# Linear attention into a gated feed-forward layer: q times kv on row halves of the TensorE array, and another order of the first two batches

## Chip, core and metric

The kernel runs on one core of a Trainium2 chip. The metric is the device time of one execution in microseconds (us). In the text, TensorE is PE in the profile, with its weight loads as PEld; VectorE is DVE, ScalarE is ACT, GpSimd is POOL, and SyncE, which issues most transfers, is SP. PSUM is the memory of eight banks that TensorE writes.

## What is computed

Attention is linear: there is no softmax. For every batch and head, k and v give a 64 x 64 matrix, q is multiplied by it, and every row of the result is divided by its root mean square. The result goes, heads side by side, as x into a gated feed-forward layer. The weights come as 64-bit floats.

```python
# q, k, v: (8 batches, 8 heads, 576, 64);  tokens: 8 * 576 = 4608, d_model 512, d_ff 1536
kv = np.einsum('bhsd,bhse->bhde', k, v)
out = np.einsum('bhsd,bhde->bhse', q, kv)
rms = np.sqrt(np.mean(out * out, axis=-1, keepdims=True) + 1e-06)
x = out / rms * g_norm                      # then (B,H,S,D) -> (B*S, H*D)
gate = 1.0 / (1.0 + np.exp(-(x @ w_gate)))
val = x @ w_val
y = gate * val @ w_out
```

## The kernel before

**Pairs.** Attention goes by pairs of heads: four pairs per batch, 32 in all. `attention(n)` (L202) gives eleven steps for pair n: KV (12 matmuls, a head on each half of the array's columns), KV_OUT (copy to SBUF; it also issues the loads of k and v for pair n + 2), Q (six transposes of q), Q_OUT (copy; issues the load of q for pair n + 2), U (q times kv), U_SQUARE, U_SUM, U_ROOT, U_NORM (square, sum of squares, root, reciprocal and product), X (six transposes back) and X_OUT (scaled by g_norm into `xT`). TensorE does KV, Q, U and X; ScalarE Q_OUT, U_SQUARE, U_ROOT and X_OUT; VectorE KV_OUT, U_SUM and U_NORM. In U (L233), both heads of a pair stand in one 128 x 128 matrix `kvs`, zero outside two 64 x 64 blocks on its diagonal, so six matmuls with 128 rows and 128 columns do both heads.

**Chunks and blocks.** Tokens go in nine chunks of 512. A plain block of the first layer (`plain`, L361, class `Plain`) takes one chunk c and one slice f of 128 hidden columns: eight matmuls of 128 x 512 (gate and value), a sigmoid on ScalarE (`gate`) and a product on VectorE (`end`), both of them issued during the block after. Chunks 0 and 1 run in plain blocks; later chunks run in another form of the first layer (`first_layer_fast`, L457), which the change leaves alone. `second_layer` (L315) multiplies with w_out and stores.

**Weights.** A unit of weights (1 MB of 64-bit floats: gate and value slices of one f, or two slices of w_out) is loaded by `load_unit` into one of three staging buffers and made 32-bit by seven VectorE operations, `s0` to `s6` (L119 to L160), after one `Abs` on ScalarE (`take_abs`). The last one issues the load of unit u + 3. `converted(u)` issues what is left of the operations up to unit u; `convert_some(n)` issues the next n.

**Order.** Each engine works in the order in which the program issues; nothing is moved. All eight pairs of batches 0 and 1 come first, in rounds (`stage`, L386) in which three pairs are at different steps:

```python
    def stage(i, n_convert):
        do(i, KV, KV_OUT, Q, Q_OUT)
        do(i - 2, U_SUM, U_ROOT, U_NORM)
        do(i - 3, X, X_OUT)
        do(i - 1, U, U_SQUARE)
```

This phase has PSUM buffers of its own (two for KV, one for Q and X, two for U). Block (0, 0) runs among the last rounds. Then PSUM is handed over to four buffers of two banks (`two`), and blocks of chunk 0 and 1 alternate with six conversion operations in each. Attention of the later batches is fed, one step at a time, into slots between the matmuls of later layers.

Of the kernel before, what the change touches and what calls it, by code (L numbers as in the profile page):

```python
# [10 lines left out]
FP32 = mybir.dt.float32  # L11
# [3 lines left out]
ALU = mybir.AluOpType  # L15
# [8 lines left out]
def kernel(  # L24
# [48 lines left out]
    def load_q(n):  # L73
        if n >= B * NHP:
            return
        b, h0 = n // NHP, 2 * (n % NHP)
        t = sb.tile([NP, NJ, 2, HD], FP32, tag="q", name="q")
        for e in range(2):
            nc.sync.dma_start(out=t[:, :, e, :], in_=q[b, h0 + e].rearrange("(p j) d -> p j d", j=NJ))
        pairs[n]["q"] = t  # L80


# [108 lines left out]
    for kv in kvs:  # L191
        nc.vector.memset(kv, 0.0)


    xT = {}
# [6 lines left out]
    def attention(n, at_ps):  # L202

        b, m = divmod(n, NHP)
        d = {}

        def kv_mm():
            d["kv"] = ps = at_ps("kv")
            for j in range(NJ):
                js = slice(HD * j, HD * j + HD)  # L210
                for e in range(2):
                    nc.tensor.matmul(ps[HD * e:HD * e + HD, 0, 0:HD], pairs[n]["k"][:, e, js], pairs[n]["v"][:, e, js],  # L212
                                     start=(j == 0), stop=(j == NJ - 1))

        def kv_out():
            for e in range(2):
                es = slice(HD * e, HD * e + HD)
                nc.vector.tensor_copy(out=kvs[n % 2][es, es], in_=d["kv"][es, 0, 0:HD])
            load_kv(n + 2)

        def q_mm():
            d["q"] = ps = at_ps("qx")
            for j in range(NJ):
                c0 = NP * (j % JH)
                nc.tensor.transpose(ps[:, j // JH, c0:c0 + NP], pairs[n]["q"][:, j].rearrange("p e d -> p (e d)"),  # L225
                                    ident[0:NP, 0:NP])

        def q_out():
            d["qT"] = sb.tile([P, 2, JH * NP], FP32, tag="qT", name="qT")
            nc.scalar.copy(out=d["qT"], in_=d["q"][:, :, 0:JH * NP])  # L230
            load_q(n + 2)

        def u_mm():  # L233

            ps = at_ps("u")
            d["u"] = ps[0:NP, :, 0:JH * P]
            for j in range(NJ):
                c0 = P * (j % JH)
                nc.tensor.matmul(ps[0:NP, j // JH, c0:c0 + P], d["qT"][:, j // JH, NP * (j % JH):NP * (j % JH) + NP],  # L239
                                 kvs[n % 2], start=True, stop=True)  # L240

        def u_square():
            d["sq"] = sb.tile([NP, 2, JH * P], FP32, tag="sq", name="sq")
            nc.scalar.activation(out=d["sq"], in_=d["u"], func=AF.Square)

        def u_sum():
            d["ms"] = sb.tile([NP, 2, 2 * JH], FP32, tag="ms", name="ms")
            nc.vector.tensor_reduce(out=d["ms"].rearrange("p i n -> p (i n)"),
                                    in_=d["sq"].rearrange("p i (n d) -> p (i n) d", d=HD), axis=AX.X, op=ALU.add)

        def u_root():
            nc.scalar.activation(out=d["ms"], in_=d["ms"], func=AF.Sqrt, bias=eps[0:NP], scale=1.0 / HD)  # L252

        def u_norm():
            nc.vector.reciprocal(d["ms"], d["ms"])
            d["xn"] = d["sq"]
            nc.vector.tensor_tensor(out=d["xn"].rearrange("p i (n d) -> p i n d", d=HD),  # L257
                                    in0=d["u"].rearrange("p i (n d) -> p i n d", d=HD),
                                    in1=d["ms"].unsqueeze(3).to_broadcast([NP, 2, 2 * JH, HD]), op=ALU.mult)

        def x_mm():
            d["x"] = ps = at_ps("qx")
            for j in range(NJ):
                c0 = NP * (j % JH)
                nc.tensor.transpose(ps[:, j // JH, c0:c0 + NP], d["xn"][:, j // JH, P * (j % JH):P * (j % JH) + P],  # L265
                                    ident[0:NP, 0:NP])
# [16 lines left out]
    def slot():  # L283
        if fill:
            fill.popleft()()
# [42 lines left out]
                store(c, t0 + i, ot)  # L328


    def two(kind=None):
        return psum0.tile([P, 2, 512], FP32, tag="two", name="two")

    def early(kind):
        shape, bufs = {"kv": ([P, 1, 512], 2), "qx": ([P, 2, 512], 1), "u": ([P, 2, 512], 2)}[kind]
        return psum_e.tile(shape, FP32, tag=kind, name=kind, bufs=bufs)

    class Plain:


        def __init__(self, c, f, ps):
            self.c, self.f, self.ps = c, f, ps

        def mm(self, i, m):
            nc.tensor.matmul(self.ps[:, i], w[("wg", "wv")[i], self.f][:, m, :], xT[self.c][:, m, :],  # L345
# [12 lines left out]
        while late:  # L358
            late.popleft()()

    def plain(c, f, n_convert):  # L361

        converted(f)
        blk = Plain(c, f, two())
        for at in range(2 * NMT):
            i, m = divmod(at, NMT)
            blk.mm(i, m)
            slot()
# [6 lines left out]
    KV, KV_OUT, Q, Q_OUT, U, U_SQUARE, U_SUM, U_ROOT, U_NORM, X, X_OUT = range(11)  # L375
    psum_ctx = tc.tile_pool(name="psum_e", bufs=1, space=bass.MemoryType.PSUM)
    psum_e = psum_ctx.__enter__()
    NE = 2 * NHP
    a = [attention(n, early) for n in range(NE)]

    def do(n, *steps):
        if 0 <= n < NE:
            for step in steps:
                a[n][step]()

    def stage(i, n_convert):  # L386
        do(i, KV, KV_OUT, Q, Q_OUT)
        do(i - 2, U_SUM, U_ROOT, U_NORM)
        do(i - 3, X, X_OUT)
        do(i - 1, U, U_SQUARE)  # L390
        if i == 0:
            take_abs(0)
        convert_some(n_convert)
        if i + 2 == NE:
            load_unit(1)
            load_unit(2)
# [4 lines left out]
    for m in range(NMT):  # L401
        blk.mm(0, m)
    take_abs(1)
    stage(NE + 1, 1)
    for m in range(NMT):
        blk.mm(1, m)
    stage(NE + 2, 1)
    blk.gate()
    convert_some(1)
    blk.end()  # L410
    psum_ctx.__exit__(None, None, None)
# [125 lines left out]
    def mm_ps():  # L537
        return psum.tile([P, 512], FP32, tag="mm", name="mm", bufs=6)

    def at_ps(kind):  # L540
        return psum.tile([P, 2, 512], FP32, tag="at", name="at")


# [37 lines left out]
```

## Time and profile before

| what | value |
|---|---|
| median of three runs | 1197.71 us (1196.88 to 1198.85) |
| the profiled execution: time, span | 1197.71 us, 1195.9 us |
| mean granted TensorE clock | 0.994 |
| TensorE busy, of the span | 1166.5 us (98%) |
| VectorE busy, of the span | 474.2 us (40%) |
| mean of a 128 x 512 matmul record in a plain block (L345) | 602 ns |
| VectorE product at the end of a plain block (L353) | 0.69 us |
| loading ScalarE's table before a root or a sigmoid | 1.28 us |

A span runs from the first to the last instruction; the time is a little longer than the span. A 32-bit matmul leaves two records on TensorE, so 12 matmuls are x24; a transpose leaves one. Records overlap (their ends are modelled), so costs are taken from start to start. In a group of instructions, the numbers after the bar are busy time and mean duration, then the idle time of the engine before them and what ended it.

### The profile page before, as it was taken

The page shows a single profiled execution, that of the slowest core. Times are in us where ns is not written, and L with a number is a line of the kernel's source. Part 1 is how long each engine was busy: PE and PEld are TensorE (multiplying, and loading weights), DVE is VectorE, ACT ScalarE, POOL GpSimd, SP SyncE. Part 2 cuts the span into 40 slices and gives each one's busy share as a digit, 9 for nine tenths or more (in the row PEclk, how much of TensorE's full clock was granted, in tenths as well). Part 3 has the DMA queues.
Part 4 walks back from the last instruction along what each step waited for, and adds up shares of the span by engine and source line. Part 5 has one row for each costly group of instructions (what it writes and reads, how often), then busy time and mean ns, then how long its engine had stood idle before and what let it go on. Part 6 is the DMA issues. An engine that isn't in the chain of part 4 may idle for free.

```text
span 1195.9 us, 13384 instructions
## 1 busy us (share of the span) xinstructions
PE 1166.5 (98%) x5136; PEld 785.7 (66%) x5136; DVE 474.2 (40%) x845; ACT 298.6 (25%) x569; POOL 242.0 (20%) x342
## 2 busy tenths in 40 slices
PE   5889999999999999999999999999999999999998
PEld 5634444554588748884788558864888478748863
DVE  5479996112045403451244304540445035404420
ACT  3422221221134203330233114320343021102110
POOL 0000001000033303430133103420333025404410
PEclk9989999999999999999999999999999999999999
DMA  9833440220211102110112021110200000010000
GB/s 239 199 104 110 138 141 14 64 72 6 56 40 31 31 26 55 45 30 18 48 32 59 9 56 30 31 36 21 62 8 1 26 9 1 1 27 9 1 9 26
DMA packets 71582, 57.48 MB, mean 48 GB/s; under 512 B 40800, under 2 KB 65376, under 8 KB 71520
## 3 DMA queue, kind: packets, MB, share of 16 engines
q1 hardware_dynamic: 71360, 56.64, 17.9%
q8 instruction: 41, 0.67, 0.3%
q14 instruction: 21, 0.17, 0.0%
q10 hardware_dynamic: 160, 0.00, 0.0%
HBM read 47.19 MB, written 9.44 MB: 47 GB/s over the span
## 4 chain that ended last, share of the span: by engine, by line
PE 95%; ACT 2%; DMA 2%; DVE 1%; issue 0%; SPq 0%; ACTq 0%; DVEq 0%
PE mm L471 42%; PE mm L322 23%; PE two L345 14%; PE two L322 7%; PE at L239 2%; PE at L212 1%; PE at L265 1%; PE at L225 1%; PE u L239 1%; DMA q<-in_q_dram 1%; ACT L252 1%; DMA v<-in_v_dram 1%; PE u L345 1%; DVE sq L257 0%; PE two L239 0%; PE qx L225 0%
## 5 line engine op out<-in xcount | busy, mean ns | idle before, releaser
L454 POOL TENSOR_TENSOR tw<-gv 128x256 f32<-128x256 f32 x168 | 120.5, 728 | 896.6 <-PE mm L471 693.5
L322 PE MATMUL mm<-wo,gv 128*128 128x512 f32 x672 | 290.5, 592 | 0.0
L471 PE MATMUL mm<-sx,tw 128*128 128x256 f32 x1008 | 234.2, 380 | 0.0
L322 PEld LDWEIGHTS mm<-wo,gv 128*128 128x128 f32 x672 | 127.3, 190 | 155.3 <-issue 155.0
L471 PEld LDWEIGHTS mm<-sx,tw 128*128 128x128 f32 x1008 | 188.8, 190 | 24.6
L345 PE MATMUL two<-xT,gv 128*128 128x512 f32 x368 | 162.8, 602 | 3.8 <-DVE gv L353 3.8
L483 DVE TENSOR_TENSOR gv<-mm,p 128x256 f32<-128x256 f32 x84 | 35.7, 425 | 321.5 <-PE mm L471 321.5
L471 PE MATMUL mm<-xT,gv 128*128 128x256 f32 x672 | 159.7, 380 | 1.2 <-ACT sg L327 1.2
L471 PEld LDWEIGHTS mm<-xT,gv 128*128 128x128 f32 x672 | 126.0, 190 | 21.2 <-issue 2.9
L345 PEld LDWEIGHTS two<-xT,gv 128*128 128x128 f32 x368 | 70.4, 193 | 90.2 <-issue 89.7
L454 POOL TENSOR_TENSOR tw<-gv,tw 128x256 f32<-128x256 f32 x168 | 126.3, 772 | 1.1
L322 PE MATMUL two<-wo,gv 128*128 128x512 f32 x192 | 84.6, 594 | 0.0
L327 ACT COPY sg<-mm 128x512 f32<-128x512 f32 x28 | 16.4, 586 | 264.4 <-PE mm L322 264.4
L492 DVE TENSOR_TENSOR gv<-mm,p 128x256 f32<-128x256 f32 x84 | 35.7, 425 | 114.0 <-PE mm L471 114.0
L471 PE MATMUL mm<-sx,gv 128*128 128x256 f32 x336 | 79.9, 381 | 0.0
L471 PE MATMUL mm<-xT,tw 128*128 128x256 f32 x336 | 79.9, 381 | 0.0
L501 ACT ACTIVATE sg<-sg 128x256 f32<-128x256 f32 x84 | 35.0, 417 | 162.9 <-DVE sg L500 161.6
L471 PEld LDWEIGHTS mm<-sx,gv 128*128 128x128 f32 x336 | 63.0, 190 | 8.5
L471 PEld LDWEIGHTS mm<-xT,tw 128*128 128x128 f32 x336 | 63.0, 190 | 8.5
L508 DVE TENSOR_TENSOR gv<-gv,sg 128x512 f32<-128x512 f32 x84 | 66.6, 832 | 0.2
L322 PEld LDWEIGHTS two<-wo,gv 128*128 128x128 f32 x192 | 35.8, 190 | 41.8 <-issue 41.6
L477 ACT COPY p<-mm 128x256 f32<-128x256 f32 x84 | 31.3, 372 | 93.7 <-PE mm L471 93.7
(84 smaller groups left out, 820.6 us busy)
## 6 DMA issues: line engine op xcount, KB each, us to landing
k<-in_k_dram SPq DMA_DIRECT2D x32, 288.0 KB, 3.5
v<-in_v_dram SPq DMA_DIRECT2D x32, 288.0 KB, 4.3
q<-in_q_dram SPq DMA_DIRECT2D x64, 144.0 KB, 3.1
st<-in_moe_w_gate_dram SPq DMA_DIRECT2D x12, 512.0 KB, 3.7
st<-in_moe_w_val_dram SPq DMA_DIRECT2D x12, 512.0 KB, 4.8
st<-in_moe_w_out_dram SPq DMA_DIRECT2D x12, 512.0 KB, 4.4
out_dram<-sg SPq DMA_DIRECT2D x24, 192.0 KB, 2.3
out_dram<-sg SPq DMA_DIRECT2D x24, 128.0 KB, 2.3
```

Source lines behind the costliest of these rows:

```text
L212: nc.tensor.matmul(ps[HD * e:HD * e + HD, 0, 0:HD], pairs[n]["k"][:, e, js], pairs[n]["v"][:, e, js], start=(j == 0), stop=(j == NJ - 1))
L239: nc.tensor.matmul(ps[0:NP, j // JH, c0:c0 + P], d["qT"][:, j // JH, NP * (j % JH):NP * (j % JH) + NP], kvs[n % 2], start=True, stop=True)
L322: nc.tensor.matmul(ps[:, i], gv[c, f][:, ts], w["wo", f], start=(f == 0), stop=(f == NFT - 1))
L327: nc.scalar.copy(out=ot, in_=ps[:, i])
L345: nc.tensor.matmul(self.ps[:, i], w[("wg", "wv")[i], self.f][:, m, :], xT[self.c][:, m, :], start=(m == 0), stop=(m == NMT - 1), skip_grou ...
L454: nc.gpsimd.tensor_tensor(out=tw[f, i], in0=b[in0], in1=b[in1] if isinstance(in1, tuple) else tw[f, in1], op=ALU.subtract)
L471: nc.tensor.matmul(ps, wt[:, m, :], xs[:, m, :], start=(new and m == 0), stop=(m == NK - 1), skip_group_check=True)
L477: nc.scalar.copy(out=d["p1"], in_=pa)
L483: tt(out=d["h"][:, h1], in0=pb, in1=d["p1"], op=ALU.add)
L492: tt(out=d["h"][:, h2], in0=pb, in1=d["p1"], op=ALU.add)
L501: nc.scalar.activation(out=d["sg"][:, h2], in_=d["sg"][:, h2], func=AF.Sigmoid)
L508: tt(out=d["h"], in0=d["h"], in1=d["sg"], op=ALU.mult)
```

## The change

It has two parts. In the first, U takes a head on each half of the array's rows: kv of the first head lies on partitions 0 to 63 and of the second on 64 to 127 (one copy in KV_OUT, no zeros), and twelve matmuls with 64 rows and 64 columns write the two heads to different PSUM banks. The norm then writes the heads back side by side.

In the second, the order at the start is another one. Unit 0 of the weights is loaded ahead of k and v, and the first two q on ScalarE's queue. Unit 0 is converted ahead of attention. The four pairs of batch 0 come next, each round going U to norm of one pair with KV and Q of a later one behind it, and block (0, 0) is spread over the last two. The pairs of batch 1 then run inside blocks 1 to 5 of chunk 0, at fixed places between their matmuls. Blocks of chunk 0 and chunk 1 alternate from f = 6 on, and chunk 1 finishes behind. All these tiles share the four PSUM buffers of two banks.

```diff
-    load_kv(0)
-    load_q(0)
     load_unit(0)
-    load_kv(1)
-    load_q(1)
+    for n in range(2):
+        load_kv(n)
+        load_q(n, nc.scalar)
...
-    kvs = [const.tile([P, P], FP32, name=f"kv{i}") for i in range(2)]
+    kvs = [const.tile([P, HD], FP32, name=f"kv{i}") for i in range(2)]
...
         def kv_out():
-            for e in range(2):
-                es = slice(HD * e, HD * e + HD)
-                nc.vector.tensor_copy(out=kvs[n % 2][es, es], in_=d["kv"][es, 0, 0:HD])
+            nc.vector.tensor_copy(out=kvs[n % 2], in_=d["kv"][:, 0, 0:HD])
             load_kv(n + 2)
...
         def u_mm():
-            ps = at_ps("u")
-            d["u"] = ps[0:NP, :, 0:JH * P]
+            ps = at_ps()
+            d["u"] = ps[0:NP, :, 0:NJ * HD]
             for j in range(NJ):
-                c0 = P * (j % JH)
-                nc.tensor.matmul(ps[0:NP, j // JH, c0:c0 + P], d["qT"][:, j // JH, NP * (j % JH):NP * (j % JH) + NP],
-                                 kvs[n % 2], start=True, stop=True)
+                for e in range(2):
+                    es = slice(HD * e, HD * e + HD)
+                    nc.tensor.matmul(ps[0:NP, e, HD * j:HD * j + HD],
+                                     d["qT"][es, j // JH, NP * (j % JH):NP * (j % JH) + NP], kvs[n % 2][es, :],
+                                     start=True, stop=True)
...
-    for i in range(NE + 1):
-        stage(i, 3 if i < 2 else 1 if i == 2 else 0)
-    blk = Plain(0, 0, early("u"))
...
-    plain(1, 0, 7)
-    for f in range(1, NFT - 3):
-        plain(0, f, 6)
-        plain(1, f, 6)
-    for f in range(NFT - 3, NFT):
-        plain(0, f, 6)
+    take_abs(0)
+    converted(0)
+    do(0, KV, KV_OUT, Q, Q_OUT)
+    do(1, KV, KV_OUT, Q, Q_OUT)
+    load_unit(1)
+    do(0, U, U_SQUARE, U_SUM, U_ROOT, U_NORM)
+    do(2, KV, KV_OUT, Q, Q_OUT)
+    do(0, X, X_OUT)
+    do(1, U, U_SQUARE, U_SUM, U_ROOT, U_NORM)
+    do(3, KV, KV_OUT, Q, Q_OUT)
+    load_unit(2)
+    do(1, X, X_OUT)
+    do(2, U, U_SQUARE, U_SUM, U_ROOT, U_NORM)
+    blk = Plain(0, 0)
+    for i in range(2):
+        blk.mm(i, 0)
+    do(2, X, X_OUT)
+    do(3, U, U_SQUARE, U_SUM, U_ROOT, U_NORM)
+    for m in (1, 2):
+        for i in range(2):
+            blk.mm(i, m)
+    take_abs(1)
+    do(3, X, X_OUT)
+    converted(1)
+    do(4, KV, KV_OUT, Q)
+    for i in range(2):
+        blk.mm(i, 3)
+    do(4, Q_OUT)
+    late.extend([blk.gate, blk.end])
+
+    def pair_steps(p):
+        n, o = a[NHP + p] if p < NHP else None, a[NHP + p - 1] if p else None
+        slots = [[] for _ in range(2 * NMT)]
+        if n:
+            if p:
+                slots[0] += [n[KV]]
+                slots[1] += [n[KV_OUT], n[Q]]
+                slots[2] += [n[Q_OUT]]
+            slots[3] += [n[U]]
+            slots[4] += [n[U_SQUARE]]
+            slots[5] += [n[U_SUM]]
+            slots[6] += [n[U_ROOT]]
+            slots[7] += [n[U_NORM]]
+        if o:
+            slots[2] += [o[X]]
+            slots[3] = [o[X_OUT]] + slots[3]
+        return slots
+
+    for f in range(1, NHP + 2):
+        plain(0, f, 7, pair_steps(f - 1))
+    for f in range(NHP + 2, NFT):
+        plain(0, f, 5, [[]] * 8)
+        plain(1, f - NHP - 2, 5, [[]] * 8)
+    for f in range(NFT - NHP - 2, NFT - 3):
+        plain(1, f, 8, [[]] * 8)
```

In `plain`, after each of the eight matmuls, the steps for that place are issued first, then one of the gate and product left over from the block before, then the conversion operations.

More of the change, by code (lines that the diff above doesn't have):

```diff
@@ L71, in load_kv, with load_q @@
             pairs[n][name] = t
-    def load_q(n):
+    def load_q(n, queue=None):
         if n >= B * NHP:
@@ L78, in load_q @@
         for e in range(2):
-            nc.sync.dma_start(out=t[:, :, e, :], in_=q[b, h0 + e].rearrange("(p j) d -> p j d", j=NJ))
+            (queue or nc.sync).dma_start(out=t[:, :, e, :], in_=q[b, h0 + e].rearrange("(p j) d -> p j d", j=NJ))
         pairs[n]["q"] = t
@@ L190 @@
     nc.vector.memset(eps, 1e-6)
-    for kv in kvs:
-        nc.vector.memset(kv, 0.0)
     xT = {}
@@ L207, in kv_mm @@
         def kv_mm():
-            d["kv"] = ps = at_ps("kv")
+            d["kv"] = ps = at_ps()
             for j in range(NJ):
@@ L215, in kv_out @@
         def kv_out():
[L216 to L218 removed]
+            nc.vector.tensor_copy(out=kvs[n % 2], in_=d["kv"][:, 0, 0:HD])
             load_kv(n + 2)
         def q_mm():
[L222 removed]
+            d["q"] = ps = at_ps()
             for j in range(NJ):
@@ L233, in u_mm @@
         def u_mm():
-            ps = at_ps("u")
-            d["u"] = ps[0:NP, :, 0:JH * P]
+            ps = at_ps()
+            d["u"] = ps[0:NP, :, 0:NJ * HD]
             for j in range(NJ):
-                c0 = P * (j % JH)
-                nc.tensor.matmul(ps[0:NP, j // JH, c0:c0 + P], d["qT"][:, j // JH, NP * (j % JH):NP * (j % JH) + NP],
-                                 kvs[n % 2], start=True, stop=True)
+                for e in range(2):
[3 more added lines that the diff above has]
+                                     start=True, stop=True)
         def u_square():
-            d["sq"] = sb.tile([NP, 2, JH * P], FP32, tag="sq", name="sq")
+            d["sq"] = sb.tile([NP, 2, NJ * HD], FP32, tag="sq", name="sq")
             nc.scalar.activation(out=d["sq"], in_=d["u"], func=AF.Square)
         def u_sum():
-            d["ms"] = sb.tile([NP, 2, 2 * JH], FP32, tag="ms", name="ms")
+            d["ms"] = sb.tile([NP, 2, NJ], FP32, tag="ms", name="ms")
             nc.vector.tensor_reduce(out=d["ms"].rearrange("p i n -> p (i n)"),
@@ L255, in u_norm @@
             nc.vector.reciprocal(d["ms"], d["ms"])
[L256 to L259, printed above, removed]
+            d["xn"] = d["sq"].rearrange("p e f -> p (e f)")
+            nc.vector.tensor_tensor(out=d["xn"].rearrange("p (j e d) -> p e j d", e=2, d=HD),
+                                    in0=d["u"].rearrange("p e (j d) -> p e j d", d=HD),
+                                    in1=d["ms"].unsqueeze(3).to_broadcast([NP, 2, NJ, HD]), op=ALU.mult)
         def x_mm():
-            d["x"] = ps = at_ps("qx")
+            d["x"] = ps = at_ps()
             for j in range(NJ):
                 c0 = NP * (j % JH)
-                nc.tensor.transpose(ps[:, j // JH, c0:c0 + NP], d["xn"][:, j // JH, P * (j % JH):P * (j % JH) + P],
+                nc.tensor.transpose(ps[:, j // JH, c0:c0 + NP], d["xn"][:, P * j:P * j + P],
                                     ident[0:NP, 0:NP])
@@ L328, in second_layer, with two, __init__ @@
                 store(c, t0 + i, ot)
-    def two(kind=None):
+    def two():
         return psum0.tile([P, 2, 512], FP32, tag="two", name="two")
-    def early(kind):
-        shape, bufs = {"kv": ([P, 1, 512], 2), "qx": ([P, 2, 512], 1), "u": ([P, 2, 512], 2)}[kind]
-        return psum_e.tile(shape, FP32, tag=kind, name=kind, bufs=bufs)
     class Plain:
-        def __init__(self, c, f, ps):
-            self.c, self.f, self.ps = c, f, ps
+        def __init__(self, c, f):
+            self.c, self.f = c, f
+            self.ps = two()
         def mm(self, i, m):
@@ L359, in finish, with plain @@
             late.popleft()()
-    def plain(c, f, n_convert):
+    def plain(c, f, n_convert, steps=None):
         converted(f)
-        blk = Plain(c, f, two())
+        blk = Plain(c, f)
         for at in range(2 * NMT):
@@ L367, in plain @@
             blk.mm(i, m)
-            slot()
+            if steps:
+                for step in steps[at]:
+                    step()
+            if steps is None:
+                slot()
             if late:
@@ L372, in plain @@
         late.extend([blk.gate, blk.end])
[L375 to L396, printed above, removed]
@@ L398 @@
-    for i in range(NE + 1):
-        stage(i, 3 if i < 2 else 1 if i == 2 else 0)
-    blk = Plain(0, 0, early("u"))
[L401 to L411, printed above, removed]
     psum0_ctx = tc.tile_pool(name="psum0", bufs=4, space=bass.MemoryType.PSUM)
     psum0 = psum0_ctx.__enter__()
-    plain(1, 0, 7)
@@ L416, with do @@
-    for f in range(1, NFT - 3):
-        plain(0, f, 6)
-        plain(1, f, 6)
-    for f in range(NFT - 3, NFT):
-        plain(0, f, 6)
+    a = [attention(n, two) for n in range(2 * NHP)]
+    def do(n, *steps):
+        for step in steps:
+            a[n][step]()
+    KV, KV_OUT, Q, Q_OUT, U, U_SQUARE, U_SUM, U_ROOT, U_NORM, X, X_OUT = range(11)
+    take_abs(0)
[4 more added lines that the diff above has]
+    do(0, U, U_SQUARE, U_SUM, U_ROOT, U_NORM)
@@ L538, in mm_ps, with at_ps @@
         return psum.tile([P, 512], FP32, tag="mm", name="mm", bufs=6)
-    def at_ps(kind):
+    def at_ps():
         return psum.tile([P, 2, 512], FP32, tag="at", name="at")
```

## The prediction

> **What bounds the kernel now.** I read the page first, then the sums by stretch, the chain of waits, and the timelines of single engines. The page and the stretches:
>
> ```profile
> PE 1166.5 (98%) x5136; PEld 785.7 (66%) x5136; DVE 474.2 (40%) x845; ACT 298.6 (25%) x569; POOL 242.0 (20%) x342
> PE   5889999999999999999999999999999999999998
> ...
> 0.00:63.00 63.00, 41.86 (x400) 34.56 (x400) 30.91 (x55) 29.08 (x55) 0.70 (x6) 0.94 0.93 208
> 63.00:204.00 141.00, 140.92 (x322) 62.22 (x323) 125.49 (x135) 28.72 (x36) 4.30 (x7) 0.98 0.32 105
> ```
>
> TensorE bounds everything after 63 us. It idles 21 us, all of it in the first 63 us, where attention of eight pairs stands alone. From 63 to 204 us VectorE is 125 of 141 us busy (converting weights): it hides, but barely. The chain of waits shows the edges:
>
> ```profile
> 47.51 0.82 ACT sq L244
> 48.33 0.02 issue
> 48.35 0.96 DVE ms L248
> 49.31 0.02 issue
> 49.34 0.31 ACT ms L252
> ...
> 50.00 0.96 DVE sq L257
> 50.97 0.14 issue
> 51.10 3.67 PE u L345 x8
> ...
> 63.08 140.64 PE two L345 x320
> 203.72 1.72 PE two L322 x4
> ```
>
> Once U (q times kv) is done, square, sum, root, reciprocal and norm take 3.5 us before X can be transposed. Twenty first-layer blocks fill 140.64 us up to 203.72 us, my mark for the end of the part that is reordered. 3.2 us of that is a half-clock start (below), so a block is 137.4 / 20 = 6.87 us. Behind the mark the order of work is unchanged but for U itself. Of the steady attention and the clock:
>
> ```profile
> 323.45 0.92 PE L212 MATMUL at<-v,k 96*64 96x64 f32 x24
> 324.30 1.99 PE L471 MATMUL mm<-sx,tw 128*128 128x256 f32 x8
> 331.83 1.47 PE L239 MATMUL at<-kv,qT 128*96 128x128 f32 x12
> 333.14 1.89 PE L471 MATMUL mm<-xT,tw 128*128 128x256 f32 x8
> ```
>
> ```profile
> 24.89:28.30 3.41, 2.04 (x35) 1.00 1.11 320
> 28.30:31.72 3.42, 3.35 (x17) 0.50 1.21 224
> 59.02:62.44 3.42, 0.21 (x3) 1.00 0.01 2
> 62.44:65.85 3.41, 2.77 (x4) 0.50 0.00 0
> 65.85:69.26 3.41, 3.41 (x6) 0.50 0.55 166
> ```
>
> U takes 1.31 us start to start (331.83 to 333.14). The clock changes on a 3.41 us grid: a thin stretch (0.2 or 2.0 us busy) is followed by half clock until a full stretch has passed.
>
> **What the Trainium skill says.** "TensorE: Matmul & The Clock Gate", Part 1, says the clock halves after idle windows of about 3.4 us; the trace agrees (3.41 us grid), and shows it after stretches that were only partly idle too. "TensorEngine Tiling (Array Packing)", Key Properties: tiles on different rows load and multiply in parallel, and a change of tiling mode drains the array. The trace shows this for column tiles only: the two heads' kv matmuls start 6.5 ns apart, a pair every 58.3 ns, and from the end of the previous stream to the next one (323.35 to 324.30) kv costs 0.94 us, of which 12 x 58.3 ns = 0.70 is pairs and 0.24 the two drains. The clock-gate page, section LDWEIGHTS: load time goes by columns. The trace agrees: 108 ns for 128 columns (324.293 to 324.401), 55 ns for kv's 64.
>
> **The change, part by part.**
>
> 1. *U on row halves.* 6 matmuls of 128 columns become 12 of 64, a head on each row half. No row tile is in this trace. Lower bound, a pair as fast as kv's: 0.94 us. Upper bound, loads of 96 columns one after another: 96 x 0.84 = 81 ns, x 24 records = 1.94 + 0.24 drains = 2.18 us. I take two loads side by side, 81 + 5 = 86 ns a pair: 12 x 86 ns + 0.24 = 1.27 us, or 0.04 less than now. 24 pairs lie behind the mark, beside a busy TensorE, so they count in full: -1.0 us (from -8.9 to +20.9). kv's copy becomes one (-0.2 us of VectorE per pair, hidden), the norm writes in another order, same 768 elements: nothing.
>
> 2. *The order at the start.* SyncE's queue now has unit 0, kv 0, kv 1, unit 3 (issued inside unit 0's conversion), kv 2, q 2, kv 3, q 3, unit 1, kv 4, and so on; q 0 and q 1 go on ScalarE's queue. One-microsecond stretches give 345 GB/s for weights (26 and 46 us), 252 for kv (17 us), 213 for q (15 us): 3.0 us a unit (1 MB), 2.3 a kv, 1.4 a q. From first data at 2.0 us, plus 1.2 us to landing (v 1: data end 11.1, landing 12.4): unit 0 at 7.6, kv 0 at 10.4, kv 1 at 13.5, q 1 at 13.9, kv 2 at 19.4, q 2 20.8, kv 3 23.2, q 3 24.6, unit 1 27.7, pair 4 31.5.
> VectorE converts unit 0 first. Seven operations take 7.1 us (62.85 to 69.97); abs precedes them, so 15.7 us; only then the kv copy of pair 0, and U0 at 16.2 (after KV1 and Q1, at half clock). ScalarE's g_norm issue waits for q 0; that costs its table load nothing before 7.6. Now each round is a serial loop, since U(n+1) stands behind X(n): U 1.3, the 3.5 us chain, X 0.5, with KV and Q of a later pair inside. U0 ends 18.3 and its norm 22.1 (with a 1.28 us table load); X0 22.2, U1 22.8 to 24.1, norm 28.0; X1 28.1, U2 28.7 to 30.0, norm 33.6; X2 33.7, U3 34.2 to 35.5, norm 39.1. Then unit 1's conversion, 7.1 us, on which block 1 waits: T1 = 46.3 us. TensorE has X3, KV4, Q4 and two matmuls for it, to 42.9, so it idles 3.4 us.
>
> 3. *Blocks 1 to 4 with attention inside.* Each waits for the unit converted during the block before. VectorE's queue in a block: kv copy, the product of the gate, four conversion operations, sum, two conversions, reciprocal, norm, last conversion; it is in order, so the sum, which waits for U's square, holds three conversion operations. Block 2 from its start: five matmuls of 0.86 with KV5 (0.9), Q5 (0.5), X4 (0.5) between put U5 at 5.4; square from 6.95 to 7.76, sum to 8.75, two conversions to 10.7, reciprocal, norm to 11.9, last operation to 13.0, and 0.14 to the next block: 13.2 us. TensorE's own work is 10.3, so 2.9 us idle a block. Block 1, without KV and X: U at 3.5, the same tail: 11.3 us. Block 5, X alone: gate product 0.6 + 7.1: 7.75 us. Sum: 11.3 + 3 x 13.2 + 7.75 = 58.5 us. ScalarE's two table loads per block (1.28 each) fit in its gaps. The PSUM buffers, now four of two banks for all tiles, cost nothing here: each is taken again only after a square, copy or norm that ended before TensorE gets there (Q5 waits for square 4, in the block before).
>
> 4. *Clock.* The 3.4 us gap before block 1 resembles 59 to 63 us, which cost about 3 us. The four gaps of 2.9 us fall on a 3.41 us grid: in about two of three positions a stretch is left with over 2 us idle and half clock follows, for 3.4 to 6.8 us, which costs 1.7 to 3.1, say 1.4 on average with the misses: 5.6. One spell in the rounds of attention: 1.7. Sum 10.3 us, bounded by 0 and 16. It delays U and so the whole VectorE tail.
>
> 5. *The remaining 15 blocks* (chunk 0 f 6 to 11, chunk 1 f 0 to 8) are again TensorE's: 15 x 6.87 = 103.1. VectorE has 10 conversion operations and two products per two blocks (11.3 of 13.7 us), so it hides. Without that cover the last wo unit would come late at the mark; 77 operations x 1.01 + 15 x 0.6 = 87 of 103 us.
>
> Sum at the mark: 46.3 + 58.5 + 10.3 + 103.1 = 218.2 against 203.72: +14.5 us. With U's -1.0: +13.5. The profiled execution took 1197.71 around its span of 1195.9, which is the median of the runs shown; 1197.7 + 13.5 = 1211 us.
>
> **Rivals.**
> - A, as summed: 1211, its own range 1203 to 1220.
> - B, the gaps never halve the clock: +4.2 at the mark, -1.0: 1201. For it: 48.78 to 52.20 us had 1.58 us busy and stayed at full clock. Against it: two of the three other thin stretches had more busy time and did not.
> - C, U's row tiles load one after another: 1.27 becomes 2.18, +20.9 in place of -1.0: 1233. For it: a record's load (81 ns) exceeds its 53 ns of columns, and no row tile is seen here. Against it: kv's column tiles load 6.5 ns apart.
> - D, faster: U's pairs run at kv's 58.3 ns, 0.94 against 1.31 in each of 24 later pairs, -8.9 us. It decides once the start loses less than 8.9; with no spell +4.2 - 8.9 gives 1193. Against it: 96-column loads, and the spells that must stay away.
> - That the change does not do what it says: the built program has 12 row-half matmuls for each pair and the new order, so no.
>
> **How the numbers follow.** A 0.60, B 0.14, C 0.14, D 0.12. 0.2% (2.4 us) is about what a measurement of this kernel can tell from no change. A and C are slower, B slower in 0.08 and the same in 0.06, D faster in 0.11 and the same in 0.01. Faster 0.11, same 0.07, slower 0.82. The range 1197 to 1234 leaves out most of D and the worse half of C.
>
> **What would show it.** First second-layer matmul near 218 us (step 3 to 5); TensorE waits on the last conversion operation (unit 1 to 5) of about 3 us each, blocks 13 us apart (3); stretches at half clock between 40 and 100 us (4); U start to start at 1.27 us in the stream (1). I am wrong if U takes over 2 us or under 1, if the waits on conversion are below 1 us, or if T1 lies outside 43 to 51 us.

## The result, and the profile after

The changed kernel took 1213.29 us (median of four executions, 1211.31 to 1214.59); beside it the kernel before took 1198.28 us (four executions, 1196.88 to 1199.55). The ratio is 1.0124 (95% interval 1.0105 to 1.0143): slower by 1.2%, where 1211 was predicted. The profiled execution took 1214.59 us, the longest of the four; its span is 1212.8 us, 16.9 longer than before's.

The page of the kernel after, TensorE's busy time and its forty slices:

```profile
PE 1174.9 (97%) x5520; PEld 779.5 (64%) x5520; DVE 465.6 (38%) x811; ACT 309.0 (25%) x577; POOL 242.1 (20%) x342
...
PE   5879999999999999999999999999999999999998
```

TensorE is busy 8.4 us longer and idles 8.5 us longer (37.9 of 1212.8 us; 29.4 of 1195.9 before). Not all of the busy time is work: at half clock the same matmul lasts longer, as the chain below shows for U. The waits of TensorE (us in total, times, longest) say who kept it:

```profile
PE two L209 <- DMA v<-in_v_dram: 14.8, 3, 10.8
PE two L341 <- DVE gv L159: 10.3, 4, 2.6
PE two L341 <- DVE kv L213: 3.2, 1, 3.2
```

The first line is the start of the program, where KV waits for its loads (10.8 us for the first, 5.3 before). L159 is the last conversion operation: four waits of up to 2.6 us, one ahead of each of blocks 2 to 5. The third line is the wait ahead of block 1. What ended it was pair 4's small kv copy (L213), which VectorE did right behind unit 1's last conversion operation. Below are pieces of the chain of waits of the kernel after (start, duration, what): the last attention rounds, the start of block 1, the wait ahead of one such block, and the mark, which is the first matmul of the second layer:

```profile
33.19 2.12 PE two L236 x24
35.31 3.71 PE two L341 x4
39.02 0.80 PE two L264 x6
39.82 1.19 PE two L236 x24
...
51.85 5.37 PE two L341 x8
...
71.58 0.82 ACT sq L242
72.42 0.95 DVE ms L246
73.37 0.61 DVE cz L150
74.00 1.23 DVE cz L154
75.23 0.14 DVE ms L253
75.47 0.95 DVE sq L256
76.42 1.15 DVE gv L159
77.70 1.10 PE two L341 x2
...
199.64 19.74 PE two L341 x46
219.38 1.72 PE two L321 x4
```

Three things are to be seen. U (L236, 24 records) takes 2.12 us at 33.19 and 1.19 at 39.82: the first is at half clock. The block that ends at 77.70 goes square, sum, two conversion operations, reciprocal, norm, last conversion operation: that is the order in which the program issues them to VectorE. The mark lies at 219.38 us, 15.7 behind before's 203.72. Behind it the kernel takes 1.2 us more than before (993.6 against 992.4 us, both from the mark by its first record, 219.22 and 203.56, to the end of the span).

### The profile page after: what moved, and what is told of

Same layout as the page of the kernel before. It is cut to its first block, busy times and chain, and to the rows that moved or that the text cites. A ratio compares the mean times of both kernels' runs of the same rounds, so it can differ in the third digit from the quotient of the medians.

```text
span 1212.8 us, 14140 instructions
## 1 busy us (share of the span) xinstructions
PE 1174.9 (97%) x5520; PEld 779.5 (64%) x5520; DVE 465.6 (38%) x811; ACT 309.0 (25%) x577; POOL 242.1 (20%) x342
## 3 DMA queue, kind: packets, MB, share of 16 engines
q1 hardware_dynamic: 68992, 56.05, 17.4%
## 4 chain that ended last, share of the span: by engine, by line
PE 92%; DVE 3%; ACT 2%; DMA 1%; issue 1%; SPq 0%; DVEq 0%; ACTq 0%
PE mm L489 42%; PE mm L321 23%; PE two L341 13%; PE two L321 7%; PE at L236 2%; PE at L209 1%; PE at L264 1%; PE two L236 1%; PE at L220 1%; DMA q<-in_q_dram 1%; DVE sq L256 1%; DMA v<-in_v_dram 1%; PE two L209 1%; PE two L264 1%; ACT L250 1%
## 5 line engine op out<-in xcount | busy, mean ns | idle before, releaser
L341 PE MATMUL two<-xT,gv 128*128 128x512 f32 x384 | 178.9, 617 | 13.5 <-DVE gv L159 10.3
```

## The experiments

Ten kernels were run. The table gives for each the time, the ratio to the kernel before, when TensorE's clock first rises (the records hold its changes), the start of block 1 of chunk 0, the time from there to block 6, the mark by its first record, and the rest of the span. Every column but the time and the ratio is from one profiled execution. The clock's changes fall on the 3.41 us grid, whose phase differs between executions, so the columns up to the mark carry a few us of chance. How much can be seen at block 1: after, norm_next_block, filled_gaps and gate_first have the same program up to there (but for the extra matmuls of filled_gaps), and it starts at 51.8, 49.3, 50.7 and 49.6 us. The last column repeats within 0.06 us for the same form of U, but for head_major.

| kernel | us | ratio (95%) | clock rises | block 1 | 1 to 6 | mark | behind |
|---|---|---|---|---|---|---|---|
| before | 1198.28 | 1 | 18.1 | | | 203.56 | 992.38 |
| after | 1213.29 | 1.0124 (1.0105 to 1.0143) | 39.3 | 51.8 | 64.4 | 219.22 | 993.58 |
| e1_block_diag | 1211.97 | 1.0110 (1.0079 to 1.0142) | 18.2 | 50.4 | 61.8 | 215.27 | 992.36 |
| e2_rows_alone | 1208.55 | 1.0082 (1.0062 to 1.0102) | 64.1 | | | 212.94 | 993.59 |
| e3_head_major | 1237.89 | one execution | 41.2 | 54.8 | 67.3 | 225.10 | 1011.01 |
| e4_norm_next_block | 1208.13 | 1.0083 (1.0066 to 1.0100) | 35.6 | 49.3 | 56.9 | 210.97 | 993.58 |
| e5_filled_gaps | 1207.98 | 1.0090 (1.0061 to 1.0119) | 38.6 | 50.7 | 58.1 | 211.81 | 993.56 |
| e6_kv_first | 1214.41 | 1.0144 (1.0114 to 1.0173) | 35.6 | 49.5 | 67.2 | 219.68 | 993.61 |
| e8_gate_first | 1201.08 | 1.0023 (0.9988 to 1.0058) | 37.2 | 49.6 | 51.4 | 205.75 | 993.55 |
| e9_dense_beside_rows | 1201.85 | 1.0036 (1.0020 to 1.0052) | 19.2 | | | 205.87 | 993.59 |
| e7_best | 1198.90 | 1.0009 (0.9999 to 1.0019) | 18.5 | 50.4 | 50.4 | 205.39 | 992.38 |
| e10_abs_later | 1195.35 | 0.9971 (0.9961 to 0.9981) | 19.5 | 45.9 | 49.6 | 199.07 | 992.38 |

The theory at the outset: the order costs some 14 us in front of the mark, by VectorE's late operations and the half clock behind the gaps, and U on row halves is next to free.

### The two parts apart: e1_block_diag and e2_rows_alone

The first is the kernel after with U as one block-diagonal product again:

```diff
-                for e in range(2):
-                    es = slice(HD * e, HD * e + HD)
-                    nc.tensor.matmul(ps[0:NP, e, HD * j:HD * j + HD],
-                                     d["qT"][es, j // JH, NP * (j % JH):NP * (j % JH) + NP], kvs[n % 2][es, :],
-                                     start=True, stop=True)
+                c0 = P * (j % JH)
+                nc.tensor.matmul(ps[0:NP, j // JH, c0:c0 + P], d["qT"][:, j // JH, NP * (j % JH):NP * (j % JH) + NP],
+                                 kvs[n % 2], start=True, stop=True)
```

> The changed order with U put back to one block-diagonal matrix. My theory: the row halves cost 1.36 us a pair in the stream against 1.31, so the part behind the mark (first second-layer matmul to the end, 993.6 us in the changed kernel) falls by 24 x 0.05 = 1.2 us to 992.4; in front of the mark U at half clock becomes slower (2.6 against 2.2 us), so the mark moves by at most 1.5 us either way and the time stays between 1211 and 1214 us. Rival: the row halves are what costs the 15 us; then the time falls to about 1200 us.

The second is the kernel before with the opposite edit: U, copy and norm on row halves, the order as it was.

> The kernel before with U on row halves alone. My theory: behind the mark +1.2 us (992.4 to 993.6), in front of it -0.4 us for each U that runs at half clock, four of eight: the time stays within 2 us of the kernel before (1198). Rival: the row halves are the loss: 1210 us or more.

Measured: 1211.97 us (two executions, 1209.41, the profiled one, and 1214.53) and 1208.55 us. The rival's 1200 us for the first did not come: with the new order, taking the row halves away gains little. Behind the mark both came as expected (992.36 and 993.59): row halves cost 1.2 us there. In front of it the theory fell. Row halves alone moved the mark by 9.4 us in a kernel whose order is untouched, where 2 at most were expected. The two parts alone cost 11.7 and 9.4 us at the mark, together 15.7: they overlap. (The first of these is from the shorter of two executions that lie 5.1 us apart.)

The cause can be read in the timeline of TensorE (start, duration, records). First the kernel before, then rows alone:

```profile
15.12 2.77 PE L239 MATMUL u<-kv,qT 128*96 128x128 f32 x12
...
19.32 1.48 PE L239 MATMUL u<-kv,qT 128*96 128x128 f32 x12
```

```profile
15.27 2.19 PE L236 MATMUL u<-kv,qT 64*96 64x64 f32 x24
20.01 2.19 PE L236 MATMUL u<-kv,qT 64*96 64x64 f32 x24
...
57.05 2.19 PE L236 MATMUL u<-kv,qT 64*96 64x64 f32 x24
59.66 5.86 PE L343 MATMUL u<-xT,gv 128*128 128x512 f32 x8 [0.43 <-DVE sq L255]
65.86 3.62 PE L343 MATMUL u<-xT,gv 128*128 128x512 f32 x8
```

Before, U drops from 2.77 to 1.48 us when the clock rises at 18.1 us. With row halves all eight U take 2.19 us, and the clock rises only at 64.1 us, 4.4 us into the first 128 x 512 matmuls. (The clock column of the stretches shows 1.00 up to the first change, as the next fence does; the durations tell it.) It was not for want of work. The stretches of rows alone on the clock's grid, counted back from its rise (from and to, length, busy us and records of PE, PEld, DVE, ACT and POOL, then clock, DMA share and GB/s):

```profile
16.31:19.72 3.41, 3.41 (x46) 3.18 (x42) 1.91 (x3) 0.81 (x1) 0.00 (x0) 1.00 1.16 236
...
26.55:29.96 3.41, 3.41 (x46) 3.08 (x46) 0.84 (x1) 1.85 (x4) 0.00 (x0) 1.00 1.10 293
...
60.69:64.10 3.41, 3.41 (x6) 1.32 (x5) 2.90 (x5) 0.78 (x2) 0.00 (x0) 1.00 0.05 12
```

TensorE's records (the number behind the length) cover the first two stretches as fully as the last, yet only the last, all of it 128 x 512 matmuls, was followed by full clock. In all, seven of the thirteen stretches from 16.31 to 60.68 us are covered for 3.41 us, and the other six for 2.6 us or more. "TensorE: Matmul & The Clock Gate", Part 1, of the Trainium skill says that full clock comes after one busy window of about 3.4 us. Here that holds only if "busy" is not read as "covered by records".

### Is it the row halves that count too little: e9_dense_beside_rows

Rows alone, with six more 128-row matmuls ahead of each of the first eight U. What they write is overwritten by U.

```diff
+            if n < 2 * NHP:
+                for j in range(NJ):
+                    nc.tensor.matmul(ps[0:NP, 0, 0:P], d["qT"][:, j // JH, NP * (j % JH):NP * (j % JH) + NP], ident,
+                                     start=True, stop=True)
```

> The kernel before with U on row halves, plus six full 128-row matmuls of 128 columns ahead of each of the first eight U, overwritten by it. Row halves alone kept TensorE at half clock from the start to 64 us and put the mark at 212.9 us. My theory: U on row halves counts too little as activity, so the clock never rises in the attention phase; with the dense matmuls it rises near 18 us as in the kernel before, and though TensorE has 8 x 1.3 us more to do, the mark is no later than 213 us, likely near 209. Rival: row halves cost by their own waits or drains; then the extra work comes on top and the mark is 10 to 20 us later.

Measured: 1201.85 us, 6.7 less than rows alone, for 48 more matmuls. The timeline of TensorE:

```profile
15.25 2.77 PE L235 MATMUL u<-ident,qT 128*96 128x128 f32 x12
17.95 1.83 PE L240 MATMUL u<-kv,qT 64*96 64x64 f32 x24
21.10 1.48 PE L235 MATMUL u<-ident,qT 128*96 128x128 f32 x12
22.51 1.24 PE L240 MATMUL u<-kv,qT 64*96 64x64 f32 x24
```

The clock rises at 19.2 us and U takes 1.24. The table says the same in the other runs: in each of the kernels with row halves and no dense matmuls beside them, the clock first rises within 2.6 to 4.8 us of the first 128 x 512 matmuls (block 0 starts at 35.2 us in the kernel after, the rise is at 39.3); with block-diagonal U it rises at 18 to 20 us. So row halves without dense matmuls beside them leave the clock at half. What in a matmul counts (rows, columns, or both), and whether the drains between tiling modes have a part in it, wasn't tried.

### The order of the twelve matmuls: e3_head_major

```diff
-            for j in range(NJ):
-                for e in range(2):
+            for e in range(2):
+                for j in range(NJ):
```

> The changed kernel with U's twelve matmuls in the order of heads: six on the first row half, then six on the second. My theory: two heads run side by side only where neighbouring matmuls lie on different rows, so the 24 records go one after another at a weight load of 81 to 85 ns: 2.0 us and 0.34 for the two changes of mode, 1.0 us more a pair, 24 us more behind the mark and about 1240 us in all. Rival: TensorE overlaps the two halves in any order (or the two drains are the cost): U stays at 1.36 us and the time at 1213.

Measured: 1237.89 us (one execution), 1011.01 behind the mark, 17.4 more, or 0.73 us for each of the 24 pairs there. The direction and the cause held, the size came out smaller than the 24 us expected. Two groups of the stream, first in the kernel after, then in this one:

```profile
347.79 1.24 PE L236 MATMUL at<-kv,qT 64*96 64x64 f32 x24
348.96 1.35 PE L489 MATMUL mm<-xT,tw 128*128 128x256 f32 x5
```

```profile
356.58 1.96 PE L236 MATMUL at<-kv,qT 64*96 64x64 f32 x24
358.47 1.99 PE L489 MATMUL mm<-xT,tw 128*128 128x256 f32 x8
```

U goes from 1.17 us start to start to 1.89. "TensorEngine Tiling (Array Packing)", Key Properties, of the Trainium skill says that different tiles load and multiply in parallel; the trace agrees, if neighbours in the stream lie on different tiles.

### What half clock costs in the blocks: e5_filled_gaps

```diff
+        if c == 0 and 1 <= f <= NHP + 1:
+            for cols in (G, G, G if f == 1 else GH):
+                nc.tensor.matmul(blk.ps[:, 0, 0:cols], w["wg", f - 1][:, 0, :], xT[0][:, 0, 0:cols],
+                                 start=True, stop=True, skip_group_check=True)
```

The extra matmuls run while TensorE would wait ahead of blocks 1 to 5; the block overwrites their result.

> The changed kernel with two and a half to three extra 128 x 512 matmuls at the start of blocks 1 to 5, into the block's own PSUM tile and overwritten by it; they need nothing but the weights of the block before, so TensorE works where it waited for a conversion. My theory: the half-clock stretches at 52.9 (3.4 us), 90.5 (6.8) and 107.5 us (3.4) come from these gaps and cost half their length, 6.8 us less what still waits; filled, blocks 1 to 5 take 11.4, 13.2, 13.2, 13.2 and about 7.9 us, 59 us in place of 64.3, and the mark falls by 4 to 6 us. Rival: the conversions alone set the blocks' length, the clock costs nothing; then the mark stays at 219 us or rises by what the extra matmuls run over.

Measured: 1207.98 us, 5.3 less than the kernel after by the medians. The mark is 7.4 us earlier, against the longest of that kernel's executions. Of that, 1.1 is there before the first extra matmul (block 0's last four records start at 45.60 us and not at 46.70), and so is chance; 6.3 lie between blocks 1 and 6 (58.1 us against 64.4; 4 to 6 were expected). The timeline of this kernel around blocks 2 and 3:

```profile
72.08 2.31 PE L363 MATMUL two<-xT,gv 128*128 128x512 f32 x6
74.75 1.12 PE L341 MATMUL two<-xT,gv 128*128 128x512 f32 x2 [0.35 <-DVE gv L159]
...
85.18 2.31 PE L363 MATMUL two<-xT,gv 128*128 128x512 f32 x6
87.85 1.12 PE L341 MATMUL two<-xT,gv 128*128 128x512 f32 x2 [0.36 <-DVE gv L159]
```

The blocks still start 13.1 us apart (74.75, 87.85): VectorE sets that, not TensorE. What went is the half clock: from 38.6 us to the end of the work it is full. In the kernel after, the gap ahead of block 4 leaves TensorE 1.17 us of work in a stretch, and half clock follows (columns as in the stretches above):

```profile
87.10:90.51 3.41, 1.17 (x3) 0.19 (x1) 3.27 (x5) 1.95 (x3) 0.00 (x0) 1.00 0.22 52
90.51:93.93 3.42, 3.07 (x22) 1.60 (x24) 0.20 (x1) 0.00 (x0) 0.00 (x0) 0.50 0.74 255
```

The gaps ahead of blocks 2 and 3, as long, each lie across two stretches that keep 1.7 us of work or more, and the clock stays full. Between blocks 1 and 6 it is at half for four stretches (from 52.9, 90.5, 93.9 and 107.5 us), 13.65 us in all. If half of that is lost, as an estimate, it is 6.8 us, near the 6.3 measured.

### The waits on VectorE: e4_norm_next_block and e8_gate_first

In the kernel after, the sum stands in VectorE's queue ahead of three conversion operations and waits for U's square. In the first edit, sum and root go to the front of the next block, the norm to its third place, and U stands one place later:

```diff
+        if o:
+            slots[0] += [o[U_SUM], o[U_ROOT]]
...
+            slots[2] += [o[U_NORM]]
...
-            slots[3] += [n[U]]
-            slots[4] += [n[U_SQUARE]]
-            slots[5] += [n[U_SUM]]
-            slots[6] += [n[U_ROOT]]
-            slots[7] += [n[U_NORM]]
+            slots[4] += [n[U]]
+            slots[5] += [n[U_SQUARE]]
```

> The changed kernel with sum, root and norm of a pair moved into the block behind it (X follows there), so that no conversion stands behind a sum that waits for U. My theory: the waits of TensorE on the last conversion operation (2.5 to 3.2 us each) go, blocks 2 to 4 take 10.5 us in place of 13.2 to 16.2, block 1 about 8.6 in place of 12.7, block 5 about 10 in place of 8.9; with the gaps the half-clock stretches after them go. From the start of block 1 to that of block 6 about 50 us in place of 64, and a time of about 1199 us. Rival: VectorE simply has too much work in these blocks (10 us of 13); then each block still waits for its conversion and less than 5 us are won.

Measured: 1208.13 us, 5.2 less than the kernel after by the medians; 1199 had been expected. The mark of its profiled execution, the shortest of four, is 8.3 us earlier, 2.5 of it ahead of block 1, where nothing was changed. The waits on the conversion went down only from 10.3 to 6.9 us. VectorE's timeline shows the wait in its new place:

```profile
69.95 0.94 DVE L246 TENSOR_REDUCE ms<-sq 96x12 f32<-96x768 f32 x1
73.17 0.69 DVE L349 TENSOR_TENSOR gv<-two,sg 128x512 f32<-128x512 f32 x1 [2.28 <-ACT sg L346]
```

The block's product waits 2.28 us for the sigmoid. On ScalarE the root, with its table load, now stood ahead of that sigmoid, and it waits for the sum. So the second edit puts the root behind the sigmoid, and the norm one place later:

```diff
-            slots[0] += [o[U_SUM], o[U_ROOT]]
+            slots[0] += [o[U_SUM]]
+            slots[1] += [o[U_ROOT]]
...
-            slots[2] += [o[U_NORM]]
+            slots[3] += [o[U_NORM]]
```

> The same as the run with the norm in the next block, but with the root behind the sigmoid of the block before and the norm one place later: there VectorE's product waited 2.3 us in each block for a sigmoid that stood behind sum, root and a table load. My theory: blocks 2 to 4 fall from 12.0 to about 10.5 us, block 5 from 12.0 to about 10, and with the long gap before block 6 gone no half clock follows it; the mark falls from 211.0 to about 203 us. Rival: VectorE's own work bounds the blocks; then they stay at 12 us.

Measured: 1201.08 us, the mark at 205.75. Blocks 2 to 6 start at 59.6, 69.9, 80.2, 90.6 and 101.0 us, 10.3 to 10.4 apart, and the four waits ahead of blocks 2 to 5 are gone. TensorE's waits in this kernel:

```profile
PE two L341 <- DVE kv L213: 3.2, 1, 3.2
PE two L341 <- DVE gv L159: 2.7, 1, 2.7
```

The 2.7 us are a new wait, ahead of block 6 (it starts at 100.98 us), where the kernel after has none. Half clock follows it from 102.1 to 105.5 us; the expectation had it gone and the mark at 203. The two edits together take 13.0 us from blocks 1 to 5 (64.4 to 51.4): the waits on the last conversion operation shrink by 7.6 (10.3 to 2.7), and half clock between blocks 1 and 6 from 13.65 us to 3.41, which at half its length is 5.1, an estimate.

### What sets the start of block 1: e6_kv_first

Loads in the order of before, and unit 0 converted in parts between the rounds, not ahead of them (the load of unit 1 then goes one round later):

```diff
+    load_kv(0)
+    load_q(0)
     load_unit(0)
-    for n in range(2):
-        load_kv(n)
-        load_q(n, nc.scalar)
+    load_kv(1)
+    load_q(1)
...
-    take_abs(0)
-    converted(0)
     do(0, KV, KV_OUT, Q, Q_OUT)
+    take_abs(0)
+    convert_some(3)
...
```

> The changed kernel with the loads in the order of the kernel before (k, v, q of pair 0, unit 0, then pair 1, all on SyncE) and unit 0 converted in parts behind the first pairs. My theory: block 1 starts late (51.9 us) because kv of pair 2 landed at 22.3 us, behind unit 3, and because VectorE converts before the first kv copy; with kv first pair 2 is there at about 18 us and the start of block 1 comes 4 to 7 us earlier, the time about 1207. Rival: the serial rounds of the four pairs at half clock set it; then block 1 moves by less than 2 us.

Measured: 1214.41 us, no gain. KV of pair 2 ran at 18.8 us in place of 22.3, and block 1 came at 49.5, 2.4 us earlier than in the kernel after. But norm_next_block, with the loads of the kernel after, has block 1 as early (the first line is from the kernel after, the second from norm_next_block, the third from kv_first):

```profile
51.85 4.39 PE L341 MATMUL two<-xT,gv 128*128 128x512 f32 x6 [3.24 <-DVE kv L213]
49.30 6.19 PE L341 MATMUL two<-xT,gv 128*128 128x512 f32 x10 [3.24 <-DVE kv L213]
49.45 1.19 PE L342 MATMUL two<-xT,gv 128*128 128x512 f32 x1 [3.23 <-DVE kv L214]
```

In that execution KV of pair 2 ran at 19.4 us. So the new order of the loads shows no gain beyond chance, and the theory (late loads set it) fell: the rounds follow each other at half clock (U of pairs 0 to 2 at 16.7, 23.9 and 30.9 us), each waiting for the norm of the one ahead. From block 1 to 6 this kernel takes 67.2 us, with more half-clock stretches between the blocks than the kernel after.

### Putting it together: e7_best and e10_abs_later

The first takes block-diagonal U, the loads of kv_first, the places of gate_first, and starts unit 1's conversion behind pair 2's norm; of its edit against the kernel after, only the last part is shown:

```diff
+    take_abs(1)
+    convert_some(3)
     blk = Plain(0, 0)
...
-    take_abs(1)
     do(3, X, X_OUT)
```

> Edit: the kernel after, with U as one block-diagonal product again, the loads in the order of before, unit 1's conversion started behind the norm of unit 2, and the places in the blocks of the run gate_first (U one place after its conversion, the root behind the gate's sigmoid of the block before, the norm in the next block). Nothing of the computation is left out. Theory (what made the change slow is the two attention rounds and the blocks' waits for late operations on VectorE, the half clock that follows the gaps, and 1.2 us of U on row halves; no part of it is inherent in taking the attention two rounds ahead): the blocks keep their 10.4 us pitch (51.4 us from block 1 to block 6, 64.4 in the kernel after), block 1 starts at 43 to 47 us because block-diagonal U lets the clock rise at about 18 us, the first matmul of the second layer lies at 198 to 202 us (before 203.6), behind it 992.4 us: 1192 to 1196 us, some 0.3% below before. Rival (what block-diagonal U gains in the clock is lost to the gaps at the change from attention to blocks, where VectorE has four units' norms in a row): block 1 at 49 us or later, the mark at 204 or later, 1198 us or more.

Measured: 1198.90 us (22 executions) against 1197.66: not faster. The rival's numbers came out: block 1 at 50.4, mark at 205.39. ScalarE's timeline shows what held block 1:

```profile
34.64 1.10 ACT L109 ACTIVATE cz<-st 128x1024 f32<-128x1024 f32 x1
39.47 1.13 ACT L109 ACTIVATE cz<-st 128x1024 f32<-128x1024 f32 x1 [3.73 <-DMA st<-in_moe_w_val_dram]
40.49 1.03 ACT L277 ACTIVATE xT<-two,g_col 128x288 f32<-128x288 f32 x3
41.40 0.82 ACT L245 ACTIVATE sq<-two 96x768 f32<-96x768 f32 x1
```

The third conversion operation of a unit also issues the `Abs` of the next unit. Now that unit 1's conversion started earlier, that `Abs` waited 3.73 us for unit 2's transfer, with X_OUT of pair 2 and the square of pair 3 behind it. The last edit moves it, and takes pair 7's sum, root, norm and X into block 6, where VectorE has five conversion operations and not seven:

```diff
-            if u:
+            if u > 1:
                 take_abs(u + 1)
...
     do(3, X, X_OUT)
+    take_abs(2)
     converted(1)
...
+        if p > NHP:
+            o = a[NHP + p - 2]
+            return [[o[U_SUM]], [o[U_ROOT]], [], [o[U_NORM]], [], [o[X]], [o[X_OUT]], []]
```

> Edit: the kernel of the run before (block-diagonal U, loads and start of before, the root behind the gate), with the Abs of weight unit 2 issued behind the last pair's X in place of inside unit 1's conversion, where it kept ScalarE waiting 3.73 us for unit 2 with the square of pair 3 behind it, and with sum, root, norm and X of pair 7 one block later, in block 6, which has five conversion operations and not seven. Nothing of the computation is left out. Theory (these two late operations are what is left of the loss): block 1 starts 3 us earlier, at 47 to 48 us, the wait of 2.7 us ahead of block 6 and its half-clock spell go (block 1 to 6: 49 us, before 50.4 in that run), the first matmul of the second layer lies at 198 to 200 us, the time is 1191.5 to 1194 us. Rival (VectorE paces the blocks anyway, 10.2 of 10.4 us, and the clock's gaps reappear elsewhere): mark at 203 or later, 1196.5 us or more.

Measured: 1195.35 us (22 executions, 1192.01 to 1197.16) against 1198.75 for the kernel before (27 executions): ratio 0.9971 (0.9961 to 0.9981). It is faster than both. Block 1 starts 4.5 us earlier than in e7_best. The profiled execution, with its mark at 199.07, took 1193.22 us, one of the lower ones; the median lies above the expected 1191.5 to 1194. It is the new order with block-diagonal U; this order with row halves wasn't run. One part didn't come: the wait ahead of block 6 is still 2.3 us, though no half clock follows it here.

```profile
PE two L344 <- DVE gv L159: 3.4, 4, 2.3
```

## Why the prediction was right, and where it was not

**The sum.** Predicted at the mark were 218.2 us; measured, 219.38. Block 6 started at 116.2 us, where the steps add up to 46.3 + 58.5 + 10.3 = 115.1. That it is so near is partly luck: block 1 came 3.9 us late (51.85 against 46.3 and the 1.7 of one spell), and blocks 1 to 5 took 2.7 us less than 58.5 + 3 + 5.6 (64.4). Behind the mark U was put at -1.0 us and cost 1.2. Two slips in the working change little: the terms of step 3 add up to 58.65, and TensorE of the kernel before idles 29.4 us in all, of which 21 lie in the first 63 us.

**Step 3, the blocks: right, and shown.** The waits on the last conversion operation are 2.5 to 2.6 us each (2.9 predicted), blocks 2 and 3, at full clock, are 13.2 us long (64.5, 77.7, 90.9), and with the clock kept full blocks 1 to 5 take 58.1 us (58.5). That VectorE's order of issue makes the wait is shown by gate_first: the same operations in other places, and all four waits are gone, though one came up ahead of block 6.

**Step 4, the clock: right for the blocks, wrong for the rounds.** For the blocks, 3 + 5.6 us were put down; filled_gaps shows 6.3. For the attention rounds one spell of 1.7 us was put down; in fact the clock is at half until 39.3 us. No run shows what this costs by itself. Filled stretches were taken to raise the clock, as Part 1 of "TensorE: Matmul & The Clock Gate" says. Rows alone and dense_beside_rows show that stretches made of U on row halves, KV and transposes do not.

**Step 2, the start: block 1 at 51.85, outside the 43 to 51 that I had allowed.** Some of that is chance. Of the four kernels with this start, norm_next_block has KV of pair 2 at 19.4 us, where the loads had been added up to, and block 1 at 49.3; in the kernel after, KV of pair 2 waits for its v until 22.3 us, and block 1 comes 2.5 us later. But 49.3 is still 3 us more than 46.3, for the rounds run at half clock: in norm_next_block it is 6.9 us from U of pair 1 to U of pair 2 (23.76 to 30.70), where 5.9 were put down. Neither kv_first (49.5) nor block_diag (50.4) moved block 1 out of the range of these four. Loads, block-diagonal U and unit 1's conversion begun earlier gave 50.4 in e7_best, and with the `Abs` out of the way it came at 45.9 in abs_later.

**Step 1, U on row halves: wrong in sign, by a small term.** A pair of matmuls steps on every 85.0 ns (86 predicted), the two heads 6.5 ns apart, and the stream, its drains included, takes 1.26 us (1.27). What I left out is behind it: the first 128 x 256 record after the change of mode takes 320 ns to the next start, where its followers take 216. The drains were priced from kv, and there too I stopped at the next start. So the mode change costs 0.24 + 0.10 us, U 1.36 in place of 1.31, and 24 pairs give +1.2 us in place of -1.0. The column "behind" shows this in every pair of kernels that differ in U. The same section of "TensorEngine Tiling (Array Packing)", Key Properties, says that switching the mode drains the array; the trace shows what it costs here.

**Step 5** (15 blocks in 103.1 us): measured 103.0, VectorE hidden.

Of the rivals, B (no half clock) put the mark 4.2 us late; with the clock kept full from 38.6 us on it is 8.3 us late (filled_gaps), since block 1 starts at 50.7 us there and not at 46.3. C (row tiles load in turn, 2.18 us) is near what head_major makes of U, 1.98 with its drains; D fell with 85 ns a pair. None of them had that row halves alone, in the old order, would cost 9 us.

## What to carry to other kernels

When attention or other small work is put inside blocks, read the queue of each in-order engine as the program issues it: an operation that waits for TensorE belongs behind everything that the next block needs, and that goes for ScalarE's roots and prefetching steps as well as for VectorE's sums. Judge an edit of matmul shape by what it does to the clock too, by comparing a matmul's duration at the start and in the stream. And sum a loss from the start of one stage to the start of the next, since a clock spell moves from one gap to another.

## What the hardware showed that I had not expected

- In rows alone the clock stayed at half to 64.1 us, although TensorE's records cover seven of the thirteen stretches of 3.41 us from 16.3 to 60.7 us wholly. With six 128-row matmuls more in each round it rose at 19.2 us.
- Behind a change of tiling mode, the first 128 x 256 record of the next stream takes 320 ns to the next start in place of 216.
- Twelve row-half matmuls take 1.17 us to the next start when heads alternate and 1.89 when they don't.
